# Loading wq in two bands of whole rows instead of two bands of columns

## The chip, the cores and the metric

The kernel runs on one core of a Trainium2 chip. The core has a matrix engine (PE, with its weight loads shown as PEld), three engines for elementwise work (DVE, ACT, POOL), and SP, which here only issues transfers and waits. Sixteen DMA engines move data between the chip's memory (HBM) and the core's SBUF, a memory of 128 partitions. The metric is the time of one execution in microseconds, the median of several runs.

## The reference

One token is decoded with 32 query heads over 8 cached key and value heads of 65536 positions each, all in fp32; a small two-layer network runs on the same normalized input, and both results are added to the input.

```python
xn = layernorm(x)                                    # 1 x 512
q = (xn @ wq).reshape(32 heads, 128)                 # wq: 512 x 4096
scores = q . k_cache * 128 ** -0.5                   # 8 x 65536 x 128, 4 query heads each
o = softmax(scores) . v_cache                        # 8 x 65536 x 128
y = x + o @ wo + relu(xn @ w1) @ w2                  # wo: 4096 x 512
```

k and v are 268 MB each; wq and wo are 8 MB each, w1 and w2 3.5 MB each.

## The kernel before

Two tiles of SBUF carry all large data. `ks` and `vs` each hold 64 KB in every one of the 128 partitions. Key tiles, and later w1 and w2, go through `ks`; wq, value tiles, and later wo, go through `vs`. One load of a k or v tile writes the whole tile, 128 rows of 64 KB. There are 32 steps, 4 for each of the 8 key heads; each needs one k tile and one v tile.

All large loads are issued by SP, in the order written: the loads of wq (L169), the first k tile (L170), then, once the last matmul on wq is done (L310), the first v tile, and from there k and v in turn, each when the engines have given its tile back (`k_free`, `v_free`). At the end come w1, w2 and wo (L318 to L321). So the order of the transfers is fixed by hand, and a load can be queued while the one ahead of it is still moving.

wq lies in HBM so that each of 128 rows is one run of 64 KB: row p goes to partition p of `vs`, and its 16384 numbers are 32 slices of 512. `load_slices` (L159) cuts such an array by columns: each count of the table is a number of slices, taken from all 128 rows, and each cut is one DMA with a semaphore of its own. It returns one mark (a semaphore and the value to wait for) for every slice. With `WQ = [4, 28]` the first DMA brings slices 0 to 3 and the second brings the rest.

The query projection (L277 to L285) runs one fp32 matmul for each of the 32 slices, with the normalized input spread over partitions (`xs`) as weights and the slice in `vs` as the moving operand, into four row groups of one PSUM bank. Matmul i waits for the mark of its slice. Then DVE copies the bank (L287), PE transposes it (L271), and DVE adds the four groups up into the queries (L289). The matmuls on the first k tile (L344) wait for that tile and for the queries. `Flow.need` (L51) lets an engine wait for a mark only if it has not waited for that value yet.

Of the kernel before, what the change touches and what calls it, by code (L numbers as in the profile page):

```python
# [33 lines left out]
FB = DFF // P  # L34
R = HKV
SLICES = R * G
WQ = [4, 28]
WO = [8, 8, 8, 4, 2, 1, 1]
PAIRED = 16
DIRECT = 28  # L40
# [29 lines left out]
def attention_and_mlp_kernel(  # L70
# [30 lines left out]
    te, ve, se, ge, sy = nc.tensor, nc.vector, nc.scalar, nc.gpsimd, nc.sync  # L101

    def place(name, *shape, rows=P):
        return nc.alloc_sbuf_tensor(name, [rows, *shape], F32).ap()
# [5 lines left out]
    vs = place("vs", NT * KEYS)  # L110
# [42 lines left out]
    def load(engine, name, dst, src, n=16):  # L153
        sem = nc.alloc_semaphore(name)
        engine.dma_start(dst, src).then_inc(sem, n)  # L155
        return sem, n


    def load_slices(name, src, counts):  # L159
        marks = []  # L160
        for n in counts:
            cut = slice(len(marks) * D, (len(marks) + n) * D)
            marks += [load(sy, f"{name}{len(marks)}", vs[:, cut], src[:, cut])] * n
        return marks


    with tc.tile_critical():
        x_in = load(se, "x_in", xT, x.rearrange("(p a) -> p a", p=P))
        wq_in = load_slices("wq", wq.rearrange("h (i r) a f -> (h i) (r a f)", r=R), WQ)  # L169
        sy.dma_start(ks, k[0, 0, :, : NT * KEYS]).then_inc(k_in, 16)  # L170
    tc.close()
    tc.compile()
# [11 lines left out]
    for t in (acc_o, acc_z, pm):  # L184
# [70 lines left out]
    xs_in = DV.op(  # L255
        lambda e: e.tensor_mul(
            xs, pz[:, :SLICES].unsqueeze(2).to_broadcast([P, SLICES, HKV]),
            mine.unsqueeze(1).to_broadcast([P, SLICES, HKV]),
        ),
        PE.mark,  # L260
    )
# [14 lines left out]
    cleared = DV.op(lambda e: e.memset(pr, 0.0))  # L276
    for i in range(SLICES):  # L277
        c = i % CT
        PE.op(
            lambda e: e.matmul(  # L280
                pr[32 * c : 32 * c + HKV, :], xs[:, i, :], vs[:, i * 512 : (i + 1) * 512],
                start=(i < CT), stop=(i >= SLICES - CT),
            ),
            cleared, xs_in, wq_in[i],
        )  # L285
    wq_read = PE.mark
    DV.op(lambda e: e.tensor_copy(rows, pr), PE.mark)  # L287
# [49 lines left out]
    with nc.Fori(0, STEPS, engines=[ENG.PE]):  # L337
        te.wait_ge(k_in, 16).then_inc(k_in, -16)
        te.wait_ge(q_in, 1).then_inc(q_in, -1)  # L339
        for s in range(NT):  # L340
            tile_of = (pa, pb)[s // 2 % 2][:, s % 2, :]
            for c in range(CT):
                at = (s * CT + c) * TW
                i = te.matmul(tile_of[32 * c : 32 * c + 32, :], qcur, ks[:, at : at + TW], start=True, stop=True)  # L344
# [12 lines left out]
        n = NT * SUB // WIDE  # L357
# [12 lines left out]
    with nc.Fori(0, HKV, engines=[ENG.DVE], head_slot={ENG.DVE: 110}):  # L370
        for n in range(NP):
            for s in range(0, NT, 2):
                if s == NT - 2:

                    ve.wait_ge(s_tiles, NT // 2).then_inc(k_free, 1)
                i = ve.transpose(  # L376
                    tr[:, s * SUB : (s + 2) * SUB, :].rearrange("p b i -> p (b i)"),
                    (pa, pb)[s // 2 % 2].rearrange("p i k -> p (i k)"),
                )._wait_ge(s_tiles, s // 2 + 1)
# [5 lines left out]
            i = ve.reduce_max(top, tr[:, :, :G].rearrange("p b g -> p g b"), axis=AX.X)  # L385
            if n:
                ve.drain()
                i = ve.tensor_max(m, m, mc)  # L388
# [29 lines left out]
    with nc.Fori(0, HKV, engines=[ENG.Activation]):  # L418
        for n in range(NP):
            se.wait_ge(s_bias, 1).then_inc(s_bias, -1)  # L420
            for g in range(G):
                i = se.activation(  # L422
                    wt[:, :, g], tr[:, :, g], AF.Exp, bias=bias[:, n, g : g + 1],
                    scale=scale, accum_out=part[:, n, g : g + 1],
                )
# [167 lines left out]
```

## Time and profile before

| | before |
|---|---|
| median of 3 runs | 1303.44 us (1303.35 to 1303.82) |
| the profiled execution | 1303.26 us, its span 1301.9 us |
| mean granted TensorE clock | 0.733 of full speed |
| read from HBM | 560.99 MB, 431 GB/s over the span |

The span goes from the first to the last instruction of the profiled execution. The page gives for each engine the time in which it was busy, for each DMA queue its packets and its share of the 16 DMA engines' time, and for each DMA issue the time until the data had landed. This is how loads wait in the queue: the k and v tiles of the main loop take much longer from issue to landing than a transfer alone, since they are issued while another is moving.

```profile
ks<-k SPq DMA_DIRECT2D x32, 28.8
vs<-v SPq DMA_DIRECT2D x32, 28.9
```

### The profile page before, as it was taken

How to read it: one execution, taken by the hardware profiler on the slowest of the kernel's cores; microseconds unless marked ns; L12 is line 12 of the kernel's file. 1: busy time of each engine (PE TensorE's matmuls, PEld its weight loads, DVE VectorE, ACT ScalarE, POOL GpSimd, SP SyncE). 2: the span in 40 equal slices, each digit the busy share in tenths (PEclk: the TensorE clock that was granted, in tenths of full speed). 3: DMA queues.
4: the chain of work that ended last, by engine and by line, in shares of the span. 5: the costliest groups of instructions: out<-in, count | busy, mean ns of one | idle time of the engine just before them, and what ended most of it. 6: DMA issues, size and time to landing. Idle time of an engine off the chain costs nothing. (4 is left out here: it accounts for less than half of the span.)

```text
span 1301.9 us, 10665 instructions
## 1 busy us (share of the span) xinstructions
PE 664.9 (51%) x4512; PEld 185.6 (14%) x4512; DVE 268.4 (21%) x398; ACT 76.0 (6%) x292; POOL 4.1 (0%) x22
## 2 busy tenths in 40 slices
PE   3355356455446445545545545544544644544658
PEld 1111111111111111111111111111111111111112
DVE  2221122221122222012222012222112222201222
ACT  0000000000000000000000000000000000000000
POOL 0000000000000000000000000000000000000000
PEclk9776676777677677667677677768777767767769
DMA  9999999999999999999999999999999999999998
GB/s 419 419 449 419 451 419 445 425 427 443 421 449 421 449 419 451 419 445 425 431 439 425 445 421 449 419 451 419 445 425 435 435 425 445 421 449 421 449 416 361
DMA packets 11101, 561.06 MB, mean 431 GB/s; under 512 B 1492, under 2 KB 1496, under 8 KB 1880
## 3 DMA queue, kind: packets, MB, share of 16 engines
q1 hardware_dynamic: 10944, 561.00, 99.7%
q8 instruction: 3, 0.05, 0.0%
q10 hardware_dynamic: 152, 0.00, 0.0%
q14 instruction: 2, 0.02, 0.0%
HBM read 560.99 MB, written 0.00 MB: 431 GB/s over the span
## 5 line engine op out<-in xcount | busy, mean ns | idle before, releaser
L360 PE MATMUL acc_o<-vs,wt 128*16 128x512 f32 x2048 | 296.3, 743 | 179.0 <-PEq L356 179.0
L344 PE MATMUL pa<-ks,qcur 128*32 128x512 f32 x1024 | 176.5, 822 | 323.8 <-PEq L339 323.8
L376 DVE STREAM_TRANSPOSE tr<-pa 128x1024 f32<-128x1024 f32 x64 | 80.0, 1250 | 412.9 <-PE pa L344 412.9
L344 PE MATMUL pb<-ks,qcur 128*32 128x512 f32 x1024 | 139.5, 665 | 0.0
L422 ACT ACTIVATE wt<-tr,bias 128x128 f32<-128x128 f32 x128 | 64.3, 511 | 1084.5 <-ACTq L420 1084.5
L360 PEld LDWEIGHTS acc_o<-vs,wt 128*16 128x16 f32 x2048 | 69.6, 114 | 379.0 <-issue 379.0
L344 PEld LDWEIGHTS pa<-ks,qcur 128*32 128x32 f32 x1024 | 38.9, 134 | 431.4 <-issue 422.4
L402 DVE SCALAR_TENSOR_TENSOR acc<-acc,alpha,acc_o 128x512 f32<-128x512 f32 x24 | 17.9, 747 | 353.2 <-PE acc_o L360 353.2
L376 DVE STREAM_TRANSPOSE tr<-pb 128x1024 f32<-128x1024 f32 x64 | 80.0, 1250 | 49.6 <-PE pb L344 49.6
L344 PEld LDWEIGHTS pb<-ks,qcur 128*32 128x32 f32 x1024 | 41.9, 132 | 107.8 <-issue 88.6
L349 PE MATMUL pm<-ident,m 128*4 128x128 f32 x32 | 10.3, 320 | 87.7 <-DVE m L388 67.2
L400 DVE COPY acc<-acc_o 128x512 f32<-128x512 f32 x8 | 5.5, 692 | 121.5 <-PE acc_o L360 121.5
L350 PE MATMUL pm<-dg,ones 4*128 4x4 f32 x64 | 15.4, 309 | 21.4 <-DVE dg L392 21.4
L385 DVE TENSOR_REDUCE mc<-tr 128x4 f32<-128x512 f32 x24 | 24.1, 1006 | 1.8
L422 ACT ACTIVATION_READ_ACCUMULATOR wt<-tr,bias 128x1 f32 x128 | 23.9, 187 | 0.0
L349 PEld LDWEIGHTS pm<-ident,m 128*4 128x4 f32 x32 | 2.6, 81 | 116.7 <-DVE m L388 89.0
L350 PEld LDWEIGHTS pm<-dg,ones 4*128 4x128 f32 x64 | 12.6, 245 | 29.0 <-DVE dg L392 29.0
L351 PE MATMUL pm<-dg,rowg 4*128 4x1 f32 x64 | 14.7, 296 | 0.0
L280 PE MATMUL pa<-vs,tr 128*8 128x512 f32 x64 | 9.6, 754 | 8.7 <-DMA vs<-wq 7.4
L351 PEld LDWEIGHTS pm<-dg,rowg 4*128 4x128 f32 x64 | 13.4, 258 | 0.0
L390 DVE TENSOR_REDUCE mg<-pm 4x1 f32<-4x128 f32 x32 | 8.9, 279 | 13.2 <-PE pm L349 13.2
L505 PE MATMUL acc_z<-vs,sw 128*1 128x512 f32 x56 | 10.1, 592 | 2.1 <-DMA vs<-wo 2.1
(98 smaller groups left out, 97.8 us busy)
## 6 DMA issues: line engine op xcount, KB each, us to landing
vs<-wq SPq DMA_DIRECT2D x1, 7168.0 KB, 21.3
ks<-w SPq DMA_DIRECT2D x2, 3584.0 KB, 22.4
vs<-wo SPq DMA_DIRECT2D x3, 2048.0 KB, 16.4
vs<-wq SPq DMA_DIRECT2D x1, 1024.0 KB, 4.8
vs<-wo SPq DMA_DIRECT2D x1, 1024.0 KB, 22.8
ks<-k SPq DMA_DIRECT2D x32, 28.8
vs<-v SPq DMA_DIRECT2D x32, 28.9
vs<-wo SPq DMA_DIRECT2D x1, 512.0 KB, 23.6
```

Source lines behind the costliest of these rows:

```text
L280: lambda e: e.matmul(pr[32 * c : 32 * c + HKV, :], xs[:, i, :], vs[:, i * 512 : (i + 1) * 512], start=(i < CT), stop=(i >= SLICES - CT),),
L344: i = te.matmul(tile_of[32 * c : 32 * c + 32, :], qcur, ks[:, at : at + TW], start=True, stop=True)
L349: te.transpose(pm[:G, :P], m, ident)._wait_ge(s_dve, 3).then_inc(s_max, 1)
L350: te.matmul(pm[:, P : P + G], ones[:G, :], dg[:, :G], start=True, stop=True)._wait_ge(s_dve, 4)
L351: te.matmul(pm[:, P + G : P + G + 1], rowg, dg[:, G : G + 1], start=True, stop=True).then_inc(s_max, 1)
L360: mm = te.matmul(acc_o[32 * c : 32 * c + WIDE * G, :], wt[:, i * WIDE : (i + 1) * WIDE, :].rearrange("p b g -> p (b g)"), vs[:, i * 512 : ...
L376: i = ve.transpose(tr[:, s * SUB : (s + 2) * SUB, :].rearrange("p b i -> p (b i)"), (pa, pb)[s // 2 % 2].rearrange("p i k -> p (i k)"),)._ ...
L385: i = ve.reduce_max(top, tr[:, :, :G].rearrange("p b g -> p g b"), axis=AX.X)
L390: ve.reduce_max(mg, pm[:G, :P], axis=AX.X)._wait_ge(s_max, 1)
L402: ve.scalar_tensor_tensor(flat, flat, alpha[:, n : n + 1], acc_o, op0=ALU.mult, op1=ALU.add)
L422: i = se.activation(wt[:, :, g], tr[:, :, g], AF.Exp, bias=bias[:, n, g : g + 1], scale=scale, accum_out=part[:, n, g : g + 1],)
L505: lambda e: e.matmul(acc_z[32 * c : 32 * c + 1, :], lhsT, row, start=c not in begun, stop=last),
```

## The change

The table `WQ` now counts rows, not slices. The first DMA of wq brings rows 0 to 15, all 64 KB of each, to partitions 0 to 15 of `vs`; the second brings rows 16 to 127 to the other 112 partitions. A slice is spread over all 128 rows, so every matmul of the query projection now waits for both loads. `load_slices` is still used for wo.

```diff
-WQ = [4, 28]
+WQ = [16, 112]
...
-        wq_in = load_slices("wq", wq.rearrange("h (i r) a f -> (h i) (r a f)", r=R), WQ)
+        wq_rows, wq_in = wq.rearrange("h (i r) a f -> (h i) (r a f)", r=R), []
+        for n in WQ:
+            first = sum(WQ[: len(wq_in)])
+            wq_in.append(load(sy, f"wq{first}", vs[first : first + n], wq_rows[first : first + n]))
         sy.dma_start(ks, k[0, 0, :, : NT * KEYS]).then_inc(k_in, 16)
...
-            cleared, xs_in, wq_in[i],
+            cleared, xs_in, *wq_in,
```

On SP, at the start of the program, this is the piece that differs (a row is a line of the code, an operation, destination and source, and partitions x numbers per partition; the lines behind the diff are three higher in the new code):

```order
 L167 NO_OP
-L172 UNCONDITIONAL_BRANCH
-L155 DMA vs<-wq 128x2048
-L155 DMA vs<-wq 128x14336
-L170 DMA ks<-k 128x16384
+L175 UNCONDITIONAL_BRANCH
+L155 DMA vs<-wq 16x16384
+L155 DMA vs<-wq 112x16384
+L173 DMA ks<-k 128x16384
 L167 UNCONDITIONAL_BRANCH
```

The two loads keep their sizes of 1 MB and 7 MB and their place ahead of the k load; their shapes change.

On PE, the query projection in the program of before, with what each row waits for (`wq0` and `wq4` are the semaphores of the two loads, named for their first slice):

```order
L254 MATMUL pb<-tr,octet 128x32 [waits dve]
L280 MATMUL pa<-vs,tr 8x512 [waits wq0,dve]
L280 MATMUL pa<-vs,tr 8x512 x3
L280 MATMUL pa<-vs,tr 8x512 [waits wq4]
L280 MATMUL pa<-vs,tr 8x512 x27
```

And the same place in the program of the change, where the semaphores are named for the first row:

```order
L257 MATMUL pb<-tr,octet 128x32 [waits dve]
L283 MATMUL pa<-vs,tr 8x512 [waits wq16,wq0,dve]
L283 MATMUL pa<-vs,tr 8x512 x31
L274 MATMUL pb<-ident,rows 128x128 [waits pool,dve]
L274 MATMUL pb<-ident,rows 128x128 x3
```

The order of the 32 matmuls is the same; the wait for the second load has moved from the fifth to the first.

## The prediction

> **What bounds the kernel now.** I read the page from the top: the busy shares, then the DMA line of the 40 slices, then the DMA queues.
>
> ```profile
> span 1301.9 us, 10665 instructions
> PE 664.9 (51%) x4512; PEld 185.6 (14%) x4512; DVE 268.4 (21%) x398; ACT 76.0 (6%) x292; POOL 4.1 (0%) x22
> ...
> DMA  9999999999999999999999999999999999999998
> ...
> q1 hardware_dynamic: 10944, 561.00, 99.7%
> ```
>
> No compute engine is busy for much more than half the span, and the 16 DMA engines are busy in every slice. The queue row gives their pace: 561.00 MB over 16 engines is 35.06 MB each, moved in 99.7% of 1301.9 us, that is in 1298.0 us. So each DMA engine moves 27.01 GB/s, a row of 64 KB (65,536 bytes) takes 2.43 us on one engine, and all 16 together move 432 GB/s. Only 0.3% of the span, 3.9 us, is left for the start and the end. The kernel is a single stream of bytes, and whatever makes an engine move its bytes more slowly is added to the end, because nothing later is idle enough to win it back.
>
> Next I read the start, which is where wq is loaded: SP's instructions in order of time, then the DMA issues, then PE around the same moments.
>
> ```profile
> 0.97 0.86 SPq L155 DMA_DIRECT2D vs<-wq  x2
> 1.89 0.42 SPq L170 DMA_DIRECT2D ks<-k  x1
> 31.11 0.35 SPq L302 DMA_DIRECT2D vs<-v  x1
> 51.82 0.34 SPq L297 DMA_DIRECT2D ks<-k  x1
> ```
>
> ```profile
> vs<-wq SPq DMA_DIRECT2D x1, 7168.0 KB, 21.3
> ...
> vs<-wq SPq DMA_DIRECT2D x1, 1024.0 KB, 4.8
> ...
> y<-yt SPq DMA_DIRECT2D x1, 2.0 KB, 1.4
> ```
>
> ```profile
> 13.49 1.89 PE L280 MATMUL pa<-vs,tr 128*8 128x512 f32 x8 [1.32 <-DVE pa L276]
> 22.80 7.74 PE L280 MATMUL pa<-vs,tr 128*8 128x512 f32 x56 [7.42 <-DMA vs<-wq]
> ...
> 42.51 2.79 PE L344 MATMUL pa<-ks,qcur 128*32 128x512 f32 x12 [10.42 <-PEq L339]
> ```
>
> All three loads are handed to the queue by 2.31 us (1.89 + 0.42). wq has landed at 22.80, when PE gets its second group; its 8 rows per engine take 8 x 2.43 = 19.4 us at the full pace, so 2.4 us between the first issue (0.97) and 22.80 are not transfer. The first k tile has landed at 42.51. The load of v is issued at 31.11, so it is queued 11.4 us before the k transfer ends: the queue does not run dry there.
>
> **The change, part by part.**
>
> *The issues.* SP still issues two wq loads and one k load, in the same order, with nothing moved past them. wq becomes 128 pieces of 64 KB, where it was 128 of 8 KB and 128 of 56 KB: 128 fewer of the 10944 packets. The queue row counts a packet's own cost as busy time, so no row separates it. What a better start could bring is bounded: of the 2.4 us above, 1.4 us is what even the 2 KB store of y takes from issue to landing. The gain lies between 0 and 1.0 us. I take 0, since the engines' bytes are the same, and keep 1.0 us for the low end.
>
> *PE's wait.* All 32 slices now wait for both loads, so the first 4 slices (8 of the 64 matmul instructions, since each fp32 matmul shows as two) no longer run at 13.49. They queue behind the second landing with the other 56. Those took 7.74 us, 0.138 us each, so 8 more add 1.1 us; behind them stand the copy at L287, the four transposes, and SP's wait at L310, which holds the load of v. That issue moves 1.1 us later than the landing of wq did, under a cover of 11.4 us. Cost 0; without the cover it would be 1.1 us.
>
> *The first load: 16 rows on 16 partitions.* In every large load of before, all 128 partitions of SBUF are written at once, and they take 432 GB/s. The new first load brings the same 1024 KB as before, but writes 16 adjacent partitions only. No row of before shows so few partitions being asked for so much. The bounds: if the engines' own 27.01 GB/s is the only limit, the load takes 2.43 us and costs 0. If the destination is the limit, the rows show no more than one eighth of 432, 54 GB/s, going into 16 partitions; 1024 KB then take 19.4 us, which costs 17.0 us. In between lies sharing: if two, four or eight engines must go through one way into SBUF that carries what one engine moves, the load costs 2.43, 7.28 (three times 2.43) or 17.0 us. The middle of the range is 8.5 us, and the step nearest to it is four to a way: **7.28 us**. All engines lose it alike, each being in its first row.
>
> [...]
>
> *The second load: 112 rows.* 112 rows are 7 for each of 16 engines, where a load of all rows gives 8. If ways into SBUF belong to fixed sets of partitions, then blocks of 7 no longer match the sets that the engines had to themselves in the loads of before, and two engines meet in one way for some of their rows; each such row takes twice as long, 2.43 us more. Bounds: none of the 7 rows, or all of them, 0 to 17.0 us. The middle is 3.5 rows. I take 3 rows for the slowest engine, **7.28 us**, since an engine that was held up in one row then runs out of step with those it met. The two upper ends don't add up: if eight engines share a way in the first load, a way serves 16 rows of 128 at 8 rows each, nearly a block of 7, and the second load then adds about one row, 17.0 + 2.4 = 19.4 us in all.
>
> [...]
>
> *Behind it.* Every later load writes all 128 partitions, 8 rows to an engine, as before, so an engine that is late stays late to the end: there are no gaps. Engines that lost less may wait for the next issue, which costs nothing, since the slowest sets each landing. The k load stands behind wq in the same queue, so landing and cover move together.
>
> *The sum.* The profiled run took 1303.26 us (its span of 1301.9 and 1.4 around it), 0.18 below the median of 1303.44. 1303.26 + 7.28 + 7.28 + 0 + 0 = **1317.8 us**, 1.1% slower.
>
> **The rivals.**
>
> *Not slower: the engines are the limit.* Place: the first load. If 16 adjacent partitions can take 432 GB/s, the 16 rows land in the time of one, the blocks of 7 meet no one, and what remains is the start: 1302.3 to 1303.3 us. It decides at the rate that 16 partitions take: at 432 GB/s nothing is lost, at half of that 2.43 us, at a quarter 7.28. For it: 27.01 GB/s on every engine looks like an engine's own pace. Against it: that pace was only ever shown with one engine to each set of 8 partitions, so the rows cannot tell whose limit it is.
>
> *The change does not do what it says.* If the partition of a row, not its place in the load, picks the engine, a few engines take the 16 rows, four or so each, and go on with fewer of the 112: 8 rows each in sum, as before. Every engine then ends as now: 1303.3 us. Against it: nothing in the rows; for it, only that later loads keep all engines level.
>
> *The first load alone costs.* If the blocks of 7 run past each other without meeting, only the first term stands: 1303.26 + 7.28 = 1310.5 us. For it: engines that were held up in step may leave it in an order that fits. Against it: 7 and 8 do not match anywhere but at the edges.
>
> *More than that.* If rows go round the engines one by one, all 16 write 16 adjacent partitions in every one of the 7 steps too, each 7.28 us longer: 1303.26 + 8 x 7.28 = 1361.5 us. With eight to a way and blocks, 1322.7 us.
>
> **How the numbers follow.** Forecast, both terms (1312 to 1320): 0.48. First term alone: 0.18. Engines are the limit: 0.20. Engine by partition: 0.05. Eight to a way: 0.04. Round the engines, or something else beyond: 0.05. The two cases near 1303 hold a quarter, so the range must reach them: from 1302.3 (the start's gain of 1.0) to 1322.7, leaving the case beyond out. The forecast's own range is 1312 to 1320. Faster or slower by over 0.2% (2.6 us, about what a measurement of this kernel can tell): a gain of 1.0 us at most leaves faster 0.02; same 0.23, from the two cases near 1303; slower 0.75.
>
> **What would show it.** The first wq load should land 4.8 + 7.3 = 12.1 us after its issue (4.8 if engines are the limit); the first matmul on wq should start at 22.80 + 14.6 = 37.4 us (30.1 with the first term alone, 22.8 with none), its 64 instructions in one group of about 8.8 us; the load of v should be issued at about 31.11 + 14.6 + 1.1 = 46.8 us, and PE still find k landing after that. The queue should count 128 packets fewer at the same megabytes. I am wrong if the first load lands in about 5 us, if the second alone carries the loss, or if the late engines win time back, so that the span grows by less than the landing of wq moved.

## The result, and the profile after

The change makes the kernel slower: 1323.83 us against 1303.43 (medians of 6 runs each), a ratio of 1.0159 with a 95% interval of 1.0148 to 1.0170. That is 20.4 us, where 14.4 had been forecast, and it lies 1.1 us above the range. The profiled execution took 1324.62 us, 21.4 more than that of before.

First the page of the kernel after: its span, its engines, the slices and the DMA queue.

```profile
span 1323.3 us, 10665 instructions
PE 655.1 (50%) x4512; PEld 183.8 (14%) x4512; DVE 268.5 (20%) x398; ACT 76.0 (6%) x292; POOL 4.1 (0%) x22
...
GB/s 210 357 442 418 438 444 420 436 444 424 432 444 428 428 444 428 428 444 430 426 444 440 418 442 442 416 442 442 416 442 444 414 442 444 420 436 444 422 427 363
...
q1 hardware_dynamic: 10816, 561.00, 99.6%
```

The line of GB/s of the kernel before, for comparison:

```profile
GB/s 419 419 449 419 451 419 445 425 427 443 421 449 421 449 419 451 419 445 425 431 439 425 445 421 449 419 451 419 445 425 435 435 425 445 421 449 421 449 416 361
```

The queue moves the same 561.00 MB in 128 packets fewer and is busy for the same share of a longer span. So the DMA engines are not idle anywhere: some of their packets take longer. By the trace's packet records (the DMA records from which the profile is made) a 64 KB row of wq takes 7.8 to 9.2 us in the first load and 3.0 to 6.4 in the second, and one of the first k tile 2.42 in the median. The line of GB/s says which: 210 and 357 in the first two slices (33 us each), against 419 and 419 before. From the third slice on it is 414 to 444, much as before (416 to 451), with a low last slice in both.

The start shows it closer: SP's instructions in order of time, then what the profile says of wq as a tile, then PE.

```profile
0.97 0.86 SPq L155 DMA_DIRECT2D vs<-wq  x2
1.89 0.42 SPq L173 DMA_DIRECT2D ks<-k  x1
55.52 0.37 SPq L305 DMA_DIRECT2D vs<-v  x1
75.27 0.34 SPq L300 DMA_DIRECT2D ks<-k  x1
```

```profile
L155 SPq DMA_DIRECT2D vs<-wq x2: 402/405/408, 1.0 to 1.4; - x2
...
DMA to landing us min/median/max: 12.5/28.4/44.3
```

```profile
45.82 9.13 PE L283 MATMUL pa<-vs,tr 128*8 128x512 f32 x64 [25.45 <-DMA vs<-wq]
55.85 0.66 PE L274 MATMUL pb<-ident,rows 128*128 128x128 f32 x4 [0.90 <-DVE rows L290]
65.32 3.64 PE L347 MATMUL pa<-ks,qcur 128*32 128x512 f32 x16 [8.81 <-PEq L342]
```

The issues stand where they stood, at 0.97 and 1.89. But the first load lands 12.5 us after its issue (4.8 before), the second 44.3 us after (21.3 before), and PE has all of wq at 45.82 instead of 22.80, 23.0 us later. Everything behind moves along: the first k tile is ready at 65.32 (42.51 before). The second k load is issued at 75.27, 23.5 us later than before, and the span ends 21.4 us later. The whole loss is in the two loads of wq.

### The profile page after: what moved, and what is told of

It reads as the page before. It is cut to its first block, busy times and chain, and to the rows that moved or that the text cites. A ratio compares the mean times of both kernels' runs of the same rounds, so it can differ in the third digit from the quotient of the medians.

```text
span 1323.3 us, 10665 instructions
## 1 busy us (share of the span) xinstructions
PE 655.1 (50%) x4512; PEld 183.8 (14%) x4512; DVE 268.5 (20%) x398; ACT 76.0 (6%) x292; POOL 4.1 (0%) x22
## 3 DMA queue, kind: packets, MB, share of 16 engines
q1 hardware_dynamic: 10816, 561.00, 99.6%
## 5 line engine op out<-in xcount | busy, mean ns | idle before, releaser
L363 PE MATMUL acc_o<-vs,wt 128*16 128x512 f32 x2048 | 292.5, 735 | 183.2 <-PEq L359 183.2
L347 PE MATMUL pb<-ks,qcur 128*32 128x512 f32 x1024 | 136.8, 652 | 0.0
L379 DVE STREAM_TRANSPOSE tr<-pb 128x1024 f32<-128x1024 f32 x64 | 80.0, 1250 | 46.8 <-PE pb L347 46.8
L353 PE MATMUL pm<-dg,ones 4*128 4x4 f32 x64 | 15.0, 302 | 21.3 <-DVE dg L395 21.3
```

The source lines that it names most:

```text
L353: te.matmul(pm[:, P : P + G], ones[:G, :], dg[:, :G], start=True, stop=True)._wait_ge(s_dve, 4)
L363: mm = te.matmul(acc_o[32 * c : 32 * c + WIDE * G, :], wt[:, i * WIDE : (i + 1) * WIDE, :].rearrange("p b g -> p (b g)"), vs[:, i * 512 : ...
L379: i = ve.transpose(tr[:, s * SUB : (s + 2) * SUB, :].rearrange("p b i -> p (b i)"), (pa, pb)[s // 2 % 2].rearrange("p i k -> p (i k)"),)._ ...
```

## The experiments

Three theories stood at the start, none of them shown by a row of before. **Destination**: fixed sets of partitions share a way into SBUF, and engines that meet in one slow down. **Source**: whole rows that lie next to each other in HBM are read slowly. **Cold start**: only the first transfer is slow. Beside them stood the doubt that PE's wait, not the loads, costs the time.

### Each load by itself

Twelve loads into `ks` ahead of wq, SP waiting for each before it issues the next (A to L are lines 170 to 192; three of them are shown):

```diff
+        rows_of, probe = wq.rearrange("h (i r) a f -> (h i) (r a f)", r=R), nc.alloc_semaphore("probe")
+        sy.dma_start(ks[0:16], rows_of[0:16]).then_inc(probe, 16)
+        sy.wait_ge(probe, 16)
+        sy.dma_start(ks[0:128:8], rows_of[0:16]).then_inc(probe, 16)
+        sy.wait_ge(probe, 32)
...
+        sy.dma_start(ks[16:128], k[0, 0, 16:128, : NT * KEYS]).then_inc(probe, 16)
+        sy.wait_ge(probe, 112)
...
```

> Twelve extra loads stand ahead of wq, each issued when the one before has landed, so each one's time from issue to landing is its own; the output is unchanged and the kernel is longer by their sum. In order: A 16 rows of wq to partitions 0-15; B the same rows to partitions 0, 8, ..., 120; C the same rows to partitions 0, 4, ..., 60; D 16 rows of k (256 KB apart in memory) to partitions 0-15; E 112 rows of wq to partitions 16-127; F 112 rows to 0-111; G 112 rows of k to 16-127; H 128 rows of wq; I 64 rows to 0-63; J 64 rows to 64-127; K 32 rows to 0-31; L 96 rows to 0-95. Destination theory (partitions share ways into SBUF, four or so engines to a way when the partitions are adjacent): A and D about 12 us (9.7 + 2.4), B and C clearly less than A (7.2 where the 16 rows reach twice as many ways); E, F and G alike, about 33 us; H 21.8; I and J each at half rate, 4 rows x 4.85 + 2.4 = 22 us. Source theory (whole rows that lie next to each other in memory are read slowly): A, B and C alike at about 12 us, D about 5; E 33 but G 19; H slow as well, 35 or more. Cold-start theory (only the first transfer of the program is slow): A 12, B, C and D about 5, E to G 19, H 22, I and J 12.

SP's instructions in order of time (start, duration of the issue, line). Since each issue waits for the landing before it, the step from one start to the next is the time of one load:

```profile
0.97 0.40 SPq L170 DMA_DIRECT2D ks<-wq  x1
12.72 0.62 SPq L172 DMA_DIRECT2D ks<-wq  x1
20.67 0.50 SPq L174 DMA_DIRECT2D ks<-wq  x1
28.10 0.33 SPq L176 DMA_DIRECT2D ks<-k  x1
39.35 0.32 SPq L178 DMA_DIRECT2D ks<-wq  x1
72.84 0.31 SPq L180 DMA_DIRECT2D ks<-wq  x1
105.58 0.31 SPq L182 DMA_DIRECT2D ks<-k  x1
138.64 0.35 SPq L184 DMA_DIRECT2D ks<-wq  x1
160.57 0.50 SPq L186 DMA_DIRECT2D ks<-wq  x1
183.43 0.48 SPq L188 DMA_DIRECT2D ks<-wq  x1
206.02 0.32 SPq L190 DMA_DIRECT2D ks<-wq  x1
218.31 0.32 SPq L192 DMA_DIRECT2D ks<-wq  x1
250.24 0.82 SPq L155 DMA_DIRECT2D vs<-wq  x2
```

A, 16 rows to partitions 0-15, takes 11.75 us; D, the same with a source 256 KB apart, 11.25; B and C, the same 16 rows to every eighth and every fourth partition, 7.95 and 7.43. So the destination sets the time of these loads, not the source, and not a cold start. H, all 128 rows, takes 21.9 us, that is 8 rows x 2.43 and 2.5 us around them. The 112 rows (E, F, G) take 33.5, 32.7 and 33.1 us, wherever they come from, against 7 x 2.43 + 2.5 = 19.5. Half of the partitions (I, J) runs at half the rate, 22.9 and 22.6 us for half the bytes of H. K, 32 rows, takes 12.3 us, and L, 96 rows, 31.9: both at half the rate as well, once the 2.5 us around a load are taken off.

By these, the first load of the change loses 11.75 - 2.5 - 2.43 = 6.8 us and the second 33.5 - 19.5 = 14.0, in sum 20.8: the size of the result. The 33 us that the expectation gives for E under the destination theory was written when the result was known; it does not follow from the three rows that the prediction doubled, which give 19.5 + 7.28 = 26.8. If only engines that meet were slow, the slowest engine of E would have met another in nearly six of its seven rows (14.0 / 2.43 = 5.8). Which engines meet, no run shows.

The packet records show what the engines did. Each load runs in steps, all 16 engines taking a row each; this is the median over the 16 engines, step by step. The first line is the second load of the change itself, the others are probes.

```
                          us per row, step by step (median of 16 engines)
change, 16-127            5.35  4.69  3.24  3.81  4.65  4.76  4.52
E  112 rows to 16-127     4.57  4.74  3.45  3.27  4.56  4.64  4.49
F  112 rows to 0-111      4.43  4.76  4.73  3.34  3.42  4.63  4.70
L   96 rows to 0-95       4.75  5.12  4.86  5.10  4.74  5.10
H  128 rows               3.13  2.42  2.42  2.42  2.42  2.42  2.42  2.42
```

The two fast steps are the third and the fourth in the loads to 16-127, the fourth and the fifth in the load to 0-111: they move by one step when the load moves by 16 partitions. The first row of the change is longer, 5.35 us; there some engines are still in the first load. In the second step of E the fastest of the 16 engines took 4.67 us. So that step is slow on all sixteen, not on a few. By these medians a row takes 3.2 to 3.8 us in the two fast steps, 4.4 to 4.8 in the other steps of the 112-row loads (the change's first row aside), and 4.7 to 5.1 in L. In the third step of E two rows took 4.56 us and the other fourteen 3.1 to 3.7, against 2.42 in H; but the engines start a step up to 2.5 us apart, so part of that may come from the slow steps beside it. That all sixteen can be slow at once was read from the data after the fact; the second set of probes below was made to test it.

### PE's wait alone

```diff
-            cleared, xs_in, wq_in[i],
+            cleared, xs_in, *wq_in,
```

> The loads of before (4 and 28 slices of all rows), but every matmul of the query projection waits for both. All theories of the loads: no change, 1303.4 us within 0.5; the load of v is issued 1.1 us later than before, under a cover of 11.4 us. If the wait is what costs: up to the whole 20 us.

1303.31 us against 1303.41, a ratio of 0.9999 (0.9989 to 1.0009). The wait is hidden as the prediction had it: SP issues the load of v 1.1 us later (before: 31.11), and PE finds the first k tile at the same moment as before, 42.51.

```profile
22.93 8.73 PE L280 MATMUL pa<-vs,tr 128*8 128x512 f32 x64 [10.77 <-DMA vs<-wq]
...
42.51 2.79 PE L344 MATMUL pa<-ks,qcur 128*32 128x512 f32 x12 [9.28 <-PEq L339]
```

```profile
32.23 0.35 SPq L302 DMA_DIRECT2D vs<-v  x1
```

### Whole rows in one load

```diff
-WQ = [16, 112]
+WQ = [128]
```

> wq in one load of 128 whole rows of 64 KB, all matmuls waiting for it. Destination theory: all ways into SBUF are used as in the loads of k, 1303.4 us within 1. Source theory (adjacent whole rows are read slowly): 1303.4 plus 8 rows at 4.4 instead of 2.43 us, 1319.

1303.49 us, a ratio of 1.0000 (0.9991 to 1.0010) to before. Rows of 64 KB cost nothing in themselves, nor do they gain anything over columns; the split into 16 and 112 is what costs. The source theory falls here as well.

### Two halves

```diff
-WQ = [16, 112]
+WQ = [64, 64]
```

> wq in two loads of 64 whole rows, partitions 0-63 and 64-127. Theory that half of the partitions holds half of the ways: 8 rows at 4.85 us per engine, 1303.4 + 19.4 = 1323 us. Theory that only odd block sizes meet (7 against 8, while 4 matches): 1303.4 us. Source theory: 1319 as for one load.

1324.51 us in its one run, 21.1 more than before, close to the 19.4 forecast for half rate; odd block sizes are not the cause. 64 rows are 4 to an engine, which divides evenly, and still a row takes about 5 us on every engine by the packet records.

### The same sixteen rows, slid along the partitions

Again twelve loads in turn. The first seven put 16 rows on every fourth partition and differ only in where they start: at 32 (twice), 28, 24, 20, 8 and 0. Then come 64 rows to 32-95 and to 0-63, 80 rows to 24-103 and to 0-79, and 32 rows to 16-47:

```diff
+        sy.dma_start(ks[32:93:4], rows_of[0:16]).then_inc(probe, 16)
+        sy.wait_ge(probe, 16)
...
+        sy.dma_start(ks[24:85:4], rows_of[0:16]).then_inc(probe, 16)
+        sy.wait_ge(probe, 64)
...
+        sy.dma_start(ks[32:96], rows_of[0:64]).then_inc(probe, 16)
+        sy.wait_ge(probe, 128)
...
```

> Twelve extra loads of wq rows ahead of wq, one after the other as in the probes before, the output unchanged. Seven bring 16 rows of 64 KB, one to an engine, to every fourth partition, and differ in the first partition alone: 32 (twice, the first as warm-up), 32, 28, 24, 20, 8, 0. [...] Theory C, any load that writes fewer than 128 partitions runs at half rate wherever it lies: 7.4 for all seven, 22 for both loads of 64 rows, 27 for both of 80.

SP's instructions in order of time; the step from one start to the next is again the time of one load:

```profile
0.96 0.64 SPq L170 DMA_DIRECT2D ks<-wq  x1
6.17 0.50 SPq L172 DMA_DIRECT2D ks<-wq  x1
11.37 0.49 SPq L174 DMA_DIRECT2D ks<-wq  x1
18.56 0.49 SPq L176 DMA_DIRECT2D ks<-wq  x1
25.86 0.49 SPq L178 DMA_DIRECT2D ks<-wq  x1
33.19 0.49 SPq L180 DMA_DIRECT2D ks<-wq  x1
40.61 0.49 SPq L182 DMA_DIRECT2D ks<-wq  x1
48.07 0.54 SPq L184 DMA_DIRECT2D ks<-wq  x1
60.49 0.50 SPq L186 DMA_DIRECT2D ks<-wq  x1
83.46 0.38 SPq L188 DMA_DIRECT2D ks<-wq  x1
110.29 0.32 SPq L190 DMA_DIRECT2D ks<-wq  x1
137.83 0.31 SPq L192 DMA_DIRECT2D ks<-wq  x1
150.28 0.83 SPq L155 DMA_DIRECT2D vs<-wq  x2
```

The same 16 rows take 5.2 us from partition 32 on, 7.2 from 28, 7.3 from 24 and from 20, 7.4 and 7.5 from 8 and 0. 64 rows to partitions 32-95 take 12.4 us, to 0-63 23.0. The last load, 32 rows to partitions 16-47, takes 12.45, about as K did with 32 rows to 0-31 (12.3). The 64 rows to 32-95 end theory C, which gave 22 us for them: it is not the number of partitions but which of them. The 80 rows take 26.8 (24-103) and 27.5 us (0-79), near the half rate of 27, although 24-103 has in it all of 32-95.

The landing times of the first seven don't show how many engines are slow, since a landing is that of the slowest engine. Each packet does. From the packet records, the 16 durations of each load, sorted:

```
from 32: 2.44 2.45 2.51 2.54 2.57 2.64 2.73 2.83 2.84 2.87 2.95 3.08 3.08 3.26 3.29 3.33
from 28: 2.80 3.02 3.02 3.04 3.06 3.09 3.10 3.19 3.20 3.21 3.21 3.26 3.32 3.53 4.14 4.93
from 24: 4.25 4.26 4.33 4.37 4.45 4.57 4.70 4.76 4.78 4.86 4.87 4.91 4.99 5.07 5.13 5.21
```

In the load from 28 two engines need 4.1 and 4.9 us. The other fourteen lie some 0.3 us above the load from 32 shown here, but about level with the first rows of other fast loads (medians 3.03 in the first load from 32, 3.13 in H), so this load does not show that the rest are slowed. In the load from 24 all sixteen need 4.25 us or more, where no engine needs more than 3.51 in the first row of H. The loads from 24 and from 32 have the fourteen partitions 32, 36, ..., 84 in common, and in the load from 32 shown here no row took more than 3.33 us. Only the rows to 24 and 28 are new. Had each of the two newcomers held up one other engine, four would be slow; yet all sixteen are. Why the others are slow with them is not shown by any run here.

### Eight bands

```diff
-WQ = [16, 112]
+WQ = [16] * 8
```

> wq in eight loads of 16 adjacent whole rows. If every one of them runs as the first load of the change and nothing is won back later: 8 x 7.0 us more than before, 1303.4 + 56 = 1359 us. If only a first or cold load is slow, or late engines catch up: 1311 to 1325 us.

1359.03 us in its one run, 55.7 more than before, 6.97 for each band. By the packet records a row takes 9.4 us on every engine from the second band on. The loss of the first load is thus seen in the program itself, it repeats with every such load, and nothing of it is won back later.

### The middle half first to be fast

```diff
-WQ = [16, 112]
+WQ = [32, 64, 32]
```

> wq in three loads, rows 0-31, 32-95, 96-127, each to the partitions of the same numbers. [...] Theory C: all at half rate, as in the two halves that took 1324.5 us: 1324 us or more.

1313.98 us, a ratio of 1.0081 (1.0065 to 1.0098), 10.7 more than before, and well under the 1324 of theory C. The 64 rows in the middle, on partitions 32 to 95, run at the full rate, the others at half: by the packet records a row takes 2.42 us in the middle after a first of 3.0, and 4.6 to 5.1 in the other two loads (medians). For the 4 rows of each engine in those two that is 2.2 to 2.7 us more a row, or 8.7 to 10.7 in sum. The same rows in two halves took 1324.51. None of the placings tried here beats a load of all rows, and no version is faster than before.

## Why the prediction was wrong

*What bounds the kernel* held. The queue is busy to 99.6% after the change, and what the wq loads lose appears at the end: 23.0 us at their landing, 21.4 in the span. The prediction had named a span that grows by less than the landing as a sign of being wrong, since late engines would then have won time back. The difference of 1.6 us is there, but the packet records give it mostly another origin. The slowest engine keeps its whole delay through the load of the first k tile, whose last packet ends at 64.47 us against 41.88. In the load of the first v tile one 16 KB packet of the instruction queue (0.97 us before, 1.10 after) holds up one engine in either kernel. Before, this makes the last engine some 1.4 us later; after, it falls on an engine that is far enough ahead of the last, which it does not delay. So it is the kernel before that loses some 1.4 us there. The remaining 0.2 us stays open.

*The issues and their start: 0.* Right. One load of whole rows gives 1.0000 of before, so nothing was gained by fewer and larger pieces.

*PE's wait: 0, under a cover of 11.4 us.* Right: 0.9999 with the wait alone.

*The first load: 7.28 us, four engines to a way.* The cost was right: 6.8 us by the probe, 6.97 in the eight bands. That four engines share a way is the author's assumption; no run shows it. The load landed 12.5 us after its issue, where 12.1 was forecast. The choice among two, four and eight engines to a way was in part luck: the prediction took the step nearest to the middle of its range, and no row of before spoke for it.

*The second load: 3 rows of 7 doubled, 7.28 us.* This is the step that failed. It measured 14.0 us in the probe, and in the program 20.4 less the first load's 7.0, that is 13.4. No run shows which engines meet, or in how many of their rows, so the 3 rows stay the author's estimate. What the runs show is how many engines are slow, and in which rows. The prediction let only "two engines meet in one way for some of their rows" and argued that a held-up engine then "runs out of step with those it met". Neither is what the packets show. In every step the rows of all sixteen engines are slow, in the change 3.24 and 3.81 us in two steps and 4.52 to 5.35 in the other five (medians), and no engine gets away from the others: in the change they start each row within 3 us of one another. In the program itself every row of the seven took at least 3.0 us on every engine, 4.5 in the mean, against 2.42. So the term should have been 7 rows at some 2 us each for all engines, not 3 rows at 2.43 for some. That rows to two more partitions can go with a slowing of all sixteen engines is shown by the load from 24 (4.25 us or more); the cause of it is open. The two moments that the prediction built on this term came late with it: PE had wq at 45.82 where 37.4 was forecast, and the load of v was issued at 55.52 instead of 46.8.

*The upper end of the range.* It rested on the same idea: with eight engines to a way in the first load, "the second load then adds about one row". With 7.0 us in the first load and 13.4 in the second, which is nearer to its own bound of 17.0 than to one row, the sum of 20.4 passed 19.4. Its 1322.7 us lies nearest to the measured 1323.83, but that case is not what happened: it would have had the first load land some 17 us later than before, and it landed 7.7 later, with the greater part of the loss in the second load.

*The rivals.* "The engines are the limit" falls with A (11.75 us) against B, C and the load from 32 (7.95, 7.43 and 5.2 for the same 16 rows): a steady 2.42 us a row was seen only in loads to all 128 partitions and to 32-95. "The change does not do what it says" falls with the landing of 12.5 us. "The first load alone" falls with the 112 rows by themselves. "Round the engines" would have given 1361.5; it is close to what eight bands took, but the change did not take its rows that way, since its second load ran at 4.5 us a row and not at 9.7.

## What to carry to other kernels

A load that is cut by partitions is not a share of the full load: 16 of 128 partitions took 11.75 us for 1 MB and 112 took 33.5 us for 7, where all 128 took 21.9 for 8. Cut a large load by columns, across all partitions, if part of it is wanted early (before, 1 MB landed so 4.8 us after its issue); if it must be cut by partitions, here 64 rows to 32-95 ran at the full rate, 12.4 us, and to 0-63 and 64-127 at half, 22.9 and 22.6. And when a profile shows DMA engines fully busy, look at bytes per second as well: after the change the queue was busy to 99.6%, and the first slice moved 210 GB/s.

## What the runs showed that was not expected

In the load from 24 all sixteen engines took at least 4.25 us a row, although fourteen of its partitions are those of the load from 32 shown above, where none took more than 3.33. The load of 96 rows took 4.7 to 5.1 us a row, nearly the 5.1 of 64 rows to partitions 0-63, where every step is slow. What makes two steps of the 112-row loads faster than the rest is less clear: a row takes 3.0 us or more in them in the change and in E and F, where they stand between slow steps. And 64 partitions can take the full 432 GB/s: 64 rows to partitions 32-95 landed in 12.4 us, 4 x 2.43 and the 2.5 us around them, half of what 64 rows to 0-63 needed.
